# Issuing the products of two matrix stages in turn, one by one, in a retention-attention and two-layer feed-forward kernel

## The chip, the cores and the metric

The kernel runs on one core of one Trainium2 chip. The metric is the device time of one execution in microseconds, as the median of three runs.

## What is computed

The reference is a decayed causal attention (4 batches, 8 heads, 576 positions, 64 dimensions a head) followed by two feed-forward layers over its 2304 rows of 512 numbers. All operands come as float32 or float64 arrays and the result is float32.

```python
ret = scores * Dmat                      # scale * q k^T, times gamma**(i-j) for j <= i
x = (ret @ v) as (2304, 512)
h = x @ w_in1;  g = where(h > 0, h, exp(min(h, 0)) - 1);  x = g @ w_out1    # 512 -> 2048 -> 512
h = relu(x @ w_in2);                                      out = (h * h) @ w_out2
```

## The kernel before

The 2304 rows are cut into five token blocks (512, 512, 512, 256 and 512 rows). Each layer goes over the blocks, and in each block over 16 slices of 128 of the 2048 inner columns. One pass over one slice of one block is a step, so there are 160 steps, 80 in each layer.

A float32 product is made of three matrix products on float32r parts: each operand is a pair (hi, lo), and `mm3` (L104 to L107) issues hi times hi, hi times lo and lo times hi, all added up in one PSUM tile.

A step has these parts:

- `up` (L270) multiplies the block's input x with 128 columns of the first matrix. Four pieces of the inner dimension by three products make 12 products, all into one PSUM tile `h`, which is one bank. There are two buffers for `h`.
- The elementwise work on `h`. In layer 0, ACT takes a relu, an exp and a tanh (L283 to L285), DVE combines them (L287, L288), ACT rounds the result to the hi part of g (L101) and DVE subtracts it for the lo part (L102). In layer 1 it is one ACT relu (L290), one DVE product (L292) and the same two for the split. g has four buffers.
- `down1` or `down2` (L296, L310) multiplies g with 128 rows of the second matrix and adds that up, over all 16 slices of the block, in four PSUM tiles `acc` (two for the block of 256 rows in layer 1). These are 12 products: four tiles by three, the three of one tile one behind the other. The step's `down` is that of the step two back (`LAG = 2`, L26).
- At a block's last slice each `acc` tile is read out. In layer 0, ACT and DVE split it into a tile `x2`, which takes one of the four g buffers until a DMA has stored it. In layer 1 it is copied to a tile `o` and stored.

Products that write 512 columns are those of the four large blocks and all of `down2`; the rest write 256.

Between the ACT and the DVE part of the elementwise work, `mid` (L404) puts work that belongs to later steps: pieces of the next block's attention (its small products run on PE), and the conversion of the float64 weights to pairs of float32r (ACT, DVE and GpSimd). The first layer's weights are converted during the first block, the second layer's in blocks 1 to 3, and these are fetched and split again in block 4.

The order in which `tile_kernel` names the instructions is a priority and not yet the order of an engine's queue. The context is opened with `schedule_with_timeline_sim=True`, and its planner may take a later instruction first when it expects an earlier one to have to wait. On the chip each engine then runs its queue in the planned order. The lines that set the priority around the change are these:

```python
        up(layer, blk, f, mid)
        pend.append((layer, blk, f))
        if len(pend) > LAG:
            l, bb, ff = pend.pop(0)
            (down1, down2)[l](bb, ff)
```

Of the kernel before, what the change touches and what calls it, by code (L numbers as in the profile page):

```python
# [16 lines left out]
B, H, S, D = 4, 8, 576, 64  # L17
NT, DM, DFF = B * S, H * D, 2048
P = 128
NP = H // 2  # L20
KC = DM // P
# [3 lines left out]
NB = len(BLOCKS)  # L25
LAG = 2  # L26
WARM = 3
# What the upper word's magnitude becomes at most: what stays finite in float32r after the shift.
MOST = float(np.array([0x7F7FF000 >> 3], np.uint32).view(np.float32)[0])
# columns of the constants: identity, causal mask, then the scales of q and of k from each first position on  # L30
C_ID, C_MASK, C_S = 0, 128, 256


def chunks_of_blocks():
    """Per token block: (batch, first position, length), chunks of at most 128 positions that
    cross neither a batch nor a block."""
    out = []
    for t, n in BLOCKS:
        end, cs = t + n, []
        while t < end:  # L40
            b, s = divmod(t, S)
            n = min(P, S - s, end - t)
            cs.append((b, s, n))
            t += n
        out.append(cs)
    return out
# [11 lines left out]
def constants():  # L58
    """The decay between positions i and j is gamma**(i - j) = gamma**(i - S/2) * gamma**(S/2 - j):
    q has the first factor and k the second, so that states and scores need none."""  # L60
    c = np.zeros((P, C_ALL), np.float64)
    i = np.arange(P)
    gamma = 1.0 - 2.0 ** (-5.0 - np.arange(H))
    c[:, C_ID:C_ID + P] = np.eye(P)
    c[:, C_MASK:C_MASK + P] = i[:, None] <= i[None, :]
    for s in STARTS:
        e = (s + i - S // 2)[:, None].astype(np.float64)
        cq, ck = scale_cols(s)
        c[:, cq:cq + H] = gamma[None, :] ** e / np.sqrt(D)
        c[:, ck:ck + H] = gamma[None, :] ** -e  # L70
    return c.astype(np.float32)
# [3 lines left out]
def tile_kernel(ctx: ExitStack, tc, q, k, v, w_in1, w_out1, w_in2, w_out2, cst, out):  # L75
# [21 lines left out]

# [1 line left out]
    def split(pair_hi, pair_lo, src, eng=nc.vector):  # L99
        """src = hi + lo, each within float32r."""  # L100
        nc.scalar.copy(pair_hi, src)  # L101
        eng.tensor_tensor(out=pair_lo, in0=src, in1=pair_hi.bitcast(F32), op=ALU.subtract)  # L102
# [5 lines left out]

# [1 line left out]
    raws, f32s, w_t = {}, {}, {}  # L110
# [13 lines left out]
    def to_f32(u):  # L124
        """Round to float32: the upper word's magnitude moves up by three bits, the exponent's
        bias changes, and the sign and the rounded lower word are added to that."""
        raw = raws.pop(u)
        upper, lower = raw[:, :, 1], raw[:, :, 0]
        a = f_p.tile([P, DM], F32, tag="f", name="f")
        ai = a.bitcast(I32)  # L130
        nc.scalar.activation(lower, lower.bitcast(U32), AF.Copy, scale=2.0 ** -29)
        nc.scalar.activation(a, upper.bitcast(F32), AF.Abs, scale=2.0 ** -112)
        nc.vector.tensor_scalar_min(a, a, MOST)  # L133
        nc.vector.tensor_scalar(out=ai, in0=ai, scalar1=3, scalar2=None, op0=ALU.logical_shift_left)  # L134
        nc.vector.scalar_tensor_tensor(  # L135
            out=ai, in0=upper, scalar=-(1 << 31), in1=ai, op0=ALU.bitwise_and, op1=ALU.bitwise_or
        )
        nc.gpsimd.tensor_tensor(out=ai, in0=ai, in1=lower, op=ALU.add)  # L138
        f32s[u] = a
# [14 lines left out]

# [1 line left out]
    nat, spare = {}, {}  # L156
    x_t = {}
    blocks = chunks_of_blocks()
    chunks = [(ch, blk) for blk in range(NB) for ch in blocks[blk]]
    # chunks of the first block beside each other, in the places of weights that come late  # L160
    aside = blocks[0][1:4]
# [17 lines left out]
    def scale_chunk(ch):  # L179
        n = ch[2]  # L180
        qn, kn, _ = nat[ch]
        # VectorE converts weights during the first two blocks
        eng = nc.gpsimd if ch in blocks[0] + blocks[1] else nc.vector
        for t, c in zip((qn, kn), scale_cols(ch[1])):
            eng.tensor_tensor(
                out=t[:n], in0=t[:n], in1=cs[:n, c:c + H].unsqueeze(2).to_broadcast([n, H, D]), op=ALU.mult
            )

    def attn_pieces(ch, blk):
# [9 lines left out]
        def sbuf(name):  # L199
            if ch not in aside:  # L200
                # P1 comes when kT has been used
                return a_p.tile([P, NP, P], F32, tag="kT" if name == "P1" else name, name=name)
            return spare[ch][("qT", "kT", "P0", "P1").index(name) + 3].rearrange("s (p i) -> s p i", p=NP)
# [28 lines left out]
        def values():  # L232
            qT = live["qT"]
            _, kn, vn = nat[ch]
            ps = psum("ps_o")
            # one bank, cleared by its first product alone: the order counts
            for p in range(NP if s else 0):
# [26 lines left out]

# [1 line left out]
    g_t = {}  # L266
    acc_t = {}
    mark = [None]

    def up(layer, blk, f, mid):  # L270
        n = BLOCKS[blk][1]
        x = x_t[layer * NB + blk]
        w = w_t[layer, 0, f]
        h = ps_h.tile([P, TB], F32, tag="h", name="h")[:, :n]
        for c in range(KC):
            o = slice(c * P, (c + 1) * P)
            mm3(h, w[:, 0, o], w[:, 1, o], x[:, c, 0, :n], x[:, c, 1, :n], c == 0, c == KC - 1)
        t = t_p.tile([P, TB], F32, tag="t", name="t")[:, :n]
        g = g_p.tile([P, 2, TB], F32R, tag="g", name="g")
        if layer == 0:  # L280
            # exp(m) - 1 = (exp(m) + 1) * tanh(m / 2), which loses no digits near 0; never less than m
            e = t_p.tile([P, TB], F32, tag="e", name="e", bufs=1)[:, :n]
# [13 lines left out]
    def down1(blk, f):  # L296
        n = BLOCKS[blk][1]
        g, w = g_t.pop((blk, f)), w_t[0, 1, f]
        if f == 0:
            acc_t[blk] = [ps_acc.tile([P, TB], F32, tag="acc", name=f"acc{m}") for m in range(KC)]  # L300
        for m in range(KC):
            c = slice(m * P, (m + 1) * P)
            a = acc_t[blk][m][:, :n]
            mm3(a, w[:, 0, c], w[:, 1, c], g[:, 0, :n], g[:, 1, :n], f == 0, f == NF - 1)
            if f == NF - 1:
                x2 = g_p.tile([P, 2, TB], F32R, tag="g", name="x2")[:, :, :n]
                split(x2[:, 0], x2[:, 1], a)
                nc.sync.dma_start(out=x2s[blk][:, m], in_=x2.bitcast(F32))

    def down2(blk, f):  # L310
        t0, n = BLOCKS[blk]
        g, w = g_t.pop((blk, f)), w_t[1, 1, f]
        if f == 0:
            acc_t[blk] = [ps_acc.tile([P, DM], F32, tag="acc", name=f"acc{m}") for m in range(n // P)]
        for m in range(n // P):
            c = slice(m * P, (m + 1) * P)
            mm3(acc_t[blk][m], g[:, 0, c], g[:, 1, c], w[:, 0], w[:, 1], f == 0, f == NF - 1)
            if f == NF - 1:
# [9 lines left out]

    # the order in which the steps need the units of a layer
    units = [(0, 0)] + [u for f in range(NF) for u in ([(0, f + 1)] if f + 1 < NF else []) + [(1, f)]]  # L330
# [4 lines left out]
    nc.vector.memset(st, 0.0)  # L335
    # brings the tensor engine to its full clock while the first loads come in
    warm = ps_h.tile([P, 512], F32, tag="h", name="warm")
# [34 lines left out]
    def w1_step(n):  # L372
        """Units of the first layer's weights: n more loaded, then converted, then split."""
        for _ in range(n):
# [3 lines left out]

    # the first block's attention, its first two chunks side by side
    new_x(0)  # L380
# [22 lines left out]
    for i, (layer, blk, f) in enumerate(steps):  # L403
        def mid():  # L404
            if layer == 0 and blk < NB - 1:
                # the attention of the next block, spread over this one
                need = 3 * len(blocks[blk + 1])
# [6 lines left out]
            elif layer == 0 and i >= NF and at["f322"] < min(len(w2), (i - NF + 1) * 0.7):  # L414
                # the second layer's weights, as float32 in DRAM until there is room
                step("park", at["f322"], w2, park_w)
# [4 lines left out]

        up(layer, blk, f, mid)
        pend.append((layer, blk, f))
        if len(pend) > LAG:
            l, bb, ff = pend.pop(0)
            (down1, down2)[l](bb, ff)
        if at["f322"] == len(w2):
            step("park", 99, w2, park_w)
        # the second layer's weights take the first's places as its last block goes by
        j = i - (NB - 1) * NF  # L430
        if j >= 0:
            while at["split2"] < len(w2):
# [5 lines left out]
                step("split2", 99, w2, split_w)  # L438
        # the second layer's inputs
        if (layer, f) == (0, 1) and blk == NB - 1 or (layer, f) == (1, LAG) and blk < NB - 1:  # L440
# [3 lines left out]
    for l, bb, ff in pend:  # L444
        (down1, down2)[l](bb, ff)

# [25 lines left out]
```

## Time and profile before

| | |
|---|---|
| median of three runs | 928.78 us |
| lowest and highest run | 927.87 us, 930.71 us |
| profiled execution: span from its first to its last instruction | 926.7 us |
| median less that span | 2.1 us |
| PE busy with products | 895.6 us (97% of the span) |
| DVE busy | 488.0 us (53%) |
| ACT busy | 420.5 us (45%) |
| POOL (GpSimd) busy | 138.0 us (15%) |

The profile gives the profiled execution by its span alone; what lies around the span is taken as the 2.1 us to the median. A product's row lasts longer than the time until the next product starts, because products are pipelined. The pitch, from one start to the next, is what a product costs when the engine is full.

### The profile page before, as it was taken

The numbers are of one execution on the slowest core, as the hardware profiler recorded it, in microseconds if no ns is written. First come the engines' busy times: TensorE is split into PE (matmuls) and PEld (weight loads), VectorE is DVE, ScalarE is ACT, GpSimd is POOL, SyncE is SP. The second block draws the span as 40 slices with busy tenths as digits, with TensorE's granted clock in tenths as the row PEclk, the third lists the DMA queues.
The fourth block names the chain that finished last, engine by engine and source line by source line (L and its number), as shares of the span: only waits on it lengthen the run. The fifth ranks groups of instructions, "written<-read, shape, count | busy, mean of one in ns | idle before, by whom it ended". The sixth has DMA issues, their size and how long they took to land.

```text
span 926.7 us, 12546 instructions
## 1 busy us (share of the span) xinstructions
PE 895.6 (97%) x4934; PEld 741.2 (80%) x4934; DVE 488.0 (53%) x784; ACT 420.5 (45%) x762; POOL 138.0 (15%) x102
## 2 busy tenths in 40 slices
PE   6988788999999999999999999999999999999997
PEld 4766566878888888999888888888888888988886
DVE  4799999676656655776566542232223222323222
ACT  4576676665556565665666532222222222222221
POOL 4565555121111111211000000000000000000000
PEclk9999999999999999999999999999999999999999
DMA  9752555274434533663443420030002002100001
GB/s 227 180 159 93 159 150 158 65 230 127 113 100 173 137 91 107 220 176 122 150 126 92 159 91 1 1 137 1 0 1 91 1 1 82 55 2 23 1 1 45
DMA packets 94778, 89.09 MB, mean 96 GB/s; under 512 B 59008, under 2 KB 77568, under 8 KB 94208
## 3 DMA queue, kind: packets, MB, share of 16 engines
q1 hardware_dynamic: 94720, 88.30, 32.2%
q8 instruction: 38, 0.62, 0.3%
q14 instruction: 20, 0.16, 0.1%
HBM read 65.74 MB, written 22.54 MB: 95 GB/s over the span
## 4 chain that ended last, share of the span: by engine, by line
PE 83%; DVE 11%; issue 2%; ACT 1%; DMA 1%; POOL 1%; SPq 0%; DVEq 0%; ACTq 0%
PE acc L105 13%; PE acc L106 13%; PE acc L107 13%; PE h L105 13%; PE h L106 13%; PE h L107 13%; DVE f L133 2%; DVE f L135 2%; DVE t L287 2%; PE ps_o L242 2%; DVE f L134 1%; PE ps_s L223 1%; PE ps_t L210 1%; PE ps_o L238 1%; DVE w L102 1%
## 5 line engine op out<-in xcount | busy, mean ns | idle before, releaser
L105 PE MATMUL h<-x,w 128*128 128x512 f32 (+1 forms) x640 | 238.3, 373 | 6.5 <-DVE t L288 5.8
L107 PE MATMUL h<-x,w 128*128 128x512 f32 (+1 forms) x640 | 237.8, 372 | 1.9 <-DVE w L102 1.9
L106 PE MATMUL h<-x,w 128*128 128x512 f32 (+1 forms) x640 | 237.1, 371 | 0.0
L292 DVE SCALAR_TENSOR_TENSOR t<-h,t 128x512 f32<-128x512 f32 (+1 forms) x80 | 51.1, 639 | 229.9 <-ACT t L290 229.9
L290 ACT ACTIVATE t<-h 128x512 f32<-128x512 f32 (+1 forms) x80 | 44.5, 556 | 237.1 <-PE h L107 237.1
L101 ACT CAST g<-t 128x512 fp32r<-128x512 f32 (+1 forms) x160 | 92.4, 578 | 128.0 <-DVE t L288 65.2
L105 PEld LDWEIGHTS h<-x,w 128*128 128x128 f32 x640 | 121.3, 190 | 29.8 <-ACT e L284 3.8
L102 DVE TENSOR_TENSOR g<-t,g 128x512 fp32r<-128x512 f32 (+1 forms) x160 | 108.7, 679 | 66.3 <-ACT g L101 59.4
L107 PEld LDWEIGHTS h<-x,w 128*128 128x128 f32 x640 | 121.2, 189 | 24.7 <-DVE w L102 4.4
L106 PEld LDWEIGHTS h<-x,w 128*128 128x128 f32 x640 | 121.4, 190 | 21.1 <-DVE x L102 0.4
L138 POOL TENSOR_TENSOR f<-f,raw 128x512 int32<-128x512 int32 x64 | 94.2, 1472 | 270.6 <-DVE f L135 186.1
L106 PE MATMUL acc<-g,w 128*128 128x512 f32 (+1 forms) x320 | 119.3, 374 | 2.5 <-DVE g L102 2.5
L105 PE MATMUL acc<-g,w 128*128 128x512 f32 (+1 forms) x320 | 116.8, 381 | 4.9 <-ACT g L101 4.8
L107 PE MATMUL acc<-g,w 128*128 128x512 f32 (+1 forms) x320 | 118.1, 370 | 0.0
L105 PE MATMUL acc<-w,g 128*128 128x512 f32 x288 | 112.2, 390 | 0.0
L106 PE MATMUL acc<-w,g 128*128 128x512 f32 x288 | 112.2, 390 | 0.0
L107 PE MATMUL acc<-w,g 128*128 128x512 f32 x288 | 111.6, 389 | 0.0
L287 DVE SCALAR_TENSOR_TENSOR t<-e,t 128x512 f32<-128x512 f32 (+1 forms) x80 | 60.0, 750 | 53.6 <-ACT t L285 53.1
L105 PEld LDWEIGHTS acc<-g,w 128*128 128x128 f32 x320 | 60.0, 190 | 16.9 <-ACT g L101 5.7
L283 ACT ACTIVATE t<-h 128x512 f32<-128x512 f32 (+1 forms) x80 | 44.3, 554 | 60.6 <-PE h L107 59.6
L106 PEld LDWEIGHTS acc<-g,w 128*128 128x128 f32 x320 | 60.5, 189 | 13.8 <-DVE g L102 4.0
L107 PEld LDWEIGHTS acc<-g,w 128*128 128x128 f32 x320 | 60.4, 189 | 10.1
(62 smaller groups left out, 954.8 us busy)
## 6 DMA issues: line engine op xcount, KB each, us to landing
raw<-in_moe_w_in_dram SPq DMA_DIRECT2D x32, 512.0 KB, 4.2
raw<-in_moe_w_out_dram SPq DMA_DIRECT2D x32, 512.0 KB, 3.6
x2s<-x SPq DMA_DIRECT2D x16, 512.0 KB, 3.3
w2s<-f SPq DMA_DIRECT2D x32, 256.0 KB, 2.3
f<-w2s SPq DMA_DIRECT2D x32, 256.0 KB, 2.7
x<-x2s SPq DMA_DIRECT2D x4, 2048.0 KB, 7.9
out_dram<-o SPq DMA_DIRECT2D x18, 256.0 KB, 2.1
q<-in_q_dram SPq DMA_DIRECT2D x13, 256.0 KB, 4.3
```

Of the source, the lines that this page charges most:

```text
L101: nc.scalar.copy(pair_hi, src)
L102: eng.tensor_tensor(out=pair_lo, in0=src, in1=pair_hi.bitcast(F32), op=ALU.subtract)
L105: nc.tensor.matmul(ps, l_hi, r_hi, start=first, stop=False)
L106: nc.tensor.matmul(ps, l_hi, r_lo, start=False, stop=False)
L107: nc.tensor.matmul(ps, l_lo, r_hi, start=False, stop=last)
L133: nc.vector.tensor_scalar_min(a, a, MOST)
L135: nc.vector.scalar_tensor_tensor(out=ai, in0=upper, scalar=-(1 << 31), in1=ai, op0=ALU.bitwise_and, op1=ALU.bitwise_or)
L138: nc.gpsimd.tensor_tensor(out=ai, in0=ai, in1=lower, op=ALU.add)
L283: nc.scalar.activation(t, h, AF.Relu, scale=-1.0)
L287: nc.vector.scalar_tensor_tensor(out=t, in0=e, scalar=1.0, in1=t, op0=ALU.add, op1=ALU.mult)
L290: nc.scalar.activation(t, h, AF.Relu)
L292: nc.vector.scalar_tensor_tensor(out=t, in0=h, scalar=0.0, in1=t, op0=ALU.max, op1=ALU.mult)
```

## The change

`up` and the two `down` functions no longer issue their products one stage behind the other. Each makes a list, and a new function `interleave` issues one product of the step's `up`, then one of the `down` of two steps back, and so on: 12 and 12, or 12 and 6 in layer 1's block of 256 rows, where every second `up` product is followed by a `down` product. A product of `down` stands between any two of `up`, and the other way round.

Inside a `down` list the order is new as well. It was tile by tile (hi hi, hi lo, lo hi of tile 0, then of tile 1, and so on). It is now part by part: hi times hi of all tiles, then hi times lo of all, then lo times hi of all, so that neighbours in the list alone (after the last step, where no `up` is left) write different tiles too.

The read-out of the accumulators at a block's last slice moves to `out1` and `out2`, called after all of the step's products and after the elementwise work of its `up` and `mid`. The elementwise work and `mid` stand behind the step's 24 products, where they stood between its 12 of `up` and its 12 of `down`. The products themselves, their number, shapes and operands are the same, as are all buffers. Removed comments are left out of the diff.

```diff
+PARTS = ((0, 0), (0, 1), (1, 0))
...
+    def interleave(ups, downs):
+        n = max(len(ups), len(downs))
+        for k in range(n):
+            for of in (ups, downs):
+                for ps, l, r, first, last in of[k * len(of) // n:(k + 1) * len(of) // n]:
+                    nc.tensor.matmul(ps, l, r, start=first, stop=last)
+
-    def up(layer, blk, f, mid):
+    def up(layer, blk, f, mid, downs):
...
+        ups = []
         for c in range(KC):
             o = slice(c * P, (c + 1) * P)
-            mm3(h, w[:, 0, o], w[:, 1, o], x[:, c, 0, :n], x[:, c, 1, :n], c == 0, c == KC - 1)
+            for i, j in PARTS:
+                ups.append((h, w[:, i, o], x[:, c, j, :n], (c, i, j) == (0, *PARTS[0]), (c, i, j) == (KC - 1, *PARTS[-1])))
+        interleave(ups, downs)
...
     def down1(blk, f):
...
-        for m in range(KC):
-            c = slice(m * P, (m + 1) * P)
+        return [
+            (acc_t[blk][m][:, :n], w[:, i, m * P:(m + 1) * P], g[:, j, :n], f == 0 and (i, j) == PARTS[0], f == NF - 1 and (i, j) == PARTS[-1])
+            for i, j in PARTS for m in range(KC)
+        ]
+
+    def out1(blk, f):
+        n = BLOCKS[blk][1]
+        for m in range(KC if f == NF - 1 else 0):
             a = acc_t[blk][m][:, :n]
-            mm3(a, w[:, 0, c], w[:, 1, c], g[:, 0, :n], g[:, 1, :n], f == 0, f == NF - 1)
-            if f == NF - 1:
+            if True:
                 x2 = g_p.tile([P, 2, TB], F32R, tag="g", name="x2")[:, :, :n]
...
     def down2(blk, f):
...
+        return [
+            (acc_t[blk][m], g[:, i, m * P:(m + 1) * P], w[:, j], f == 0 and (i, j) == PARTS[0], f == NF - 1 and (i, j) == PARTS[-1])
+            for i, j in PARTS for m in range(n // P)
+        ]
+
+    def out2(blk, f):
+        t0, n = BLOCKS[blk]
         for m in range(n // P):
-            c = slice(m * P, (m + 1) * P)
-            mm3(acc_t[blk][m], g[:, 0, c], g[:, 1, c], w[:, 0], w[:, 1], f == 0, f == NF - 1)
             if f == NF - 1:
...
-        up(layer, blk, f, mid)
         pend.append((layer, blk, f))
-        if len(pend) > LAG:
-            l, bb, ff = pend.pop(0)
-            (down1, down2)[l](bb, ff)
+        done = pend.pop(0) if len(pend) > LAG else None
+        up(layer, blk, f, mid, (down1, down2)[done[0]](*done[1:]) if done else [])
+        if done:
+            (out1, out2)[done[0]](*done[1:])
...
     for l, bb, ff in pend:
-        (down1, down2)[l](bb, ff)
+        interleave([], (down1, down2)[l](bb, ff))
+        (out1, out2)[l](bb, ff)
```

## Rows read from the trace of the kernel before

**Rows 1.** The page: span, and busy time of each engine.

```profile
span 926.7 us, 12546 instructions
...
PE 895.6 (97%) x4934; PEld 741.2 (80%) x4934; DVE 488.0 (53%) x784; ACT 420.5 (45%) x762; POOL 138.0 (15%) x102
```

**Rows 2.** Windows of 23 us: window and its length, busy us by engine, granted clock, DMA.

```profile
46.00:69.00 23.00, 20.27 (x126) 15.18 (x124) 22.82 (x31) 16.79 (x31) 14.06 (x10) 1.00 0.57 159
...
161.00:184.00 23.00, 23.00 (x115) 18.79 (x114) 14.30 (x23) 13.61 (x24) 4.39 (x4) 0.99 0.20 53
...
874.00:897.00 23.00, 23.00 (x104) 19.03 (x103) 5.54 (x8) 4.88 (x8) 0.00 (x0) 1.00 0.00 1
```

**Rows 3.** Waits of PE between 40 and 161 us: total us, times, longest.

```profile
PE h L105 <- DVE t L288: 5.8, 6, 1.5
```

**Rows 4.** Groups of products by line and shape: count, busy us, mean ns.

```profile
L105 PE MATMUL h<-x,w 128*128 128x512 f32 x512 | 201.7, 394 | 6.5 <-DVE t L288 5.8 <-ACT e L284 0.4 <-ACT t L283 0.2
...
L105 PE MATMUL acc<-w,g 128*128 128x512 f32 x288 | 112.2, 390 | 0.0
...
L105 PE MATMUL acc<-g,w 128*128 128x512 f32 x256 | 99.4, 405 | 4.9 <-ACT g L101 4.8
...
L105 PE MATMUL h<-x,w 128*128 128x256 f32 x128 | 36.6, 286 | 0.0
...
L105 PE MATMUL acc<-g,w 128*128 128x256 f32 x64 | 17.4, 287 | 0.0
```

**Rows 5.** Timeline, a step of layer 1: start us, us; first products of three runs.

```profile
702.48 0.39 PE L105 MATMUL h<-x,w 128*128 128x512 f32 x1
...
705.20 0.39 PE L105 MATMUL acc<-w,g 128*128 128x512 f32 x1
...
707.92 0.39 PE L105 MATMUL h<-x,w 128*128 128x512 f32 x1
```

**Rows 6.** Timeline, the last four products of the kernel.

```profile
920.78 1.07 PE L107 MATMUL acc<-w,g 128*128 128x512 f32 x4
```

**Rows 7.** Timeline, products of 256 columns in `down1` of block 3.

```profile
440.72 0.52 PE L105 MATMUL acc<-g,w 128*128 128x256 f32 x3
...
441.80 0.28 PE L105 MATMUL acc<-g,w 128*128 128x256 f32 x1
...
442.04 0.28 PE L107 MATMUL acc<-g,w 128*128 128x256 f32 x1
```

**Rows 8.** Timeline, layer 0, block 4: a step's last `h` product, its g's hi part.

```profile
498.26 0.39 PE L107 MATMUL h<-x,w 128*128 128x512 f32 x1
...
502.47 0.62 ACT L101 CAST g<-t 128x512 fp32r<-128x512 f32 x1 [0.45 <-DVE t L288]
```

**Rows 9.** Groups by line: the longest of three DVE instructions that convert a weight unit.

```profile
L135 DVE SCALAR_TENSOR_TENSOR f<-raw,f 128x512 int32<-128x512 int32 x64 | 46.7, 730 | 0.6
```

**Rows 10.** As rows 8, in layer 0, block 3 (256 columns).

```profile
436.42 0.28 PE L107 MATMUL h<-x,w 128*128 128x256 f32 x1
...
438.97 0.41 ACT L101 CAST g<-t 128x256 fp32r<-128x256 f32 x1 [0.95 <-DVE t L288]
```

**Rows 11.** As rows 8, in layer 1, block 4.

```profile
913.30 0.39 PE L107 MATMUL h<-x,w 128*128 128x512 f32 x1
...
915.14 0.62 ACT L101 CAST g<-t 128x512 fp32r<-128x512 f32 x1 [0.76 <-DVE t L292]
```

**Rows 12.** Timeline (PE's, then ACT's), end of layer 0's first block.

```profile
176.89 0.39 PE L107 MATMUL acc<-g,w 128*128 128x512 f32 x1
...
183.88 0.39 PE L105 MATMUL acc<-g,w 128*128 128x512 f32 x1
...
181.21 1.07 ACT L101 CAST x<-acc 128x512 fp32r<-128x512 f32 x2
...
188.46 0.58 ACT L101 CAST x<-acc 128x512 fp32r<-128x512 f32 x1
```

**Rows 13.** DMA issues on the page: count, size each, median us to landing.

```profile
x2s<-x SPq DMA_DIRECT2D x16, 512.0 KB, 3.3
```

## The prediction

> **What bounds the kernel now.** The page comes first. PE is busy for 97% of the span and no other engine for more than 53% [rows 1]. A share of busy time is a mean over stages, so the windows come next. They show two stages. From 46 to about 161 us DVE is busy for 22.82 of 23 us, and PE has gaps: the first layer's weights are being converted, and DVE sets the pace. From 161 us on PE is busy for all 23 us of a window, DVE for 14.3 us and later for 5.5, at a granted clock of 0.99 to 1.00, which is the 2.4 GHz level [rows 2]. There PE sets the pace, and the view of waits has no row for PE after 161 us. Before it, PE's largest wait is 5.8 us in six pieces, for the DVE instruction that frees an `h` buffer [rows 3].
>
> So a change in the order of PE's products can act in three ways: on the pitch of a product, which counts for 766 us of the span; on waits that PE does not have now; and on DVE's pace in the first stage.
>
> The third view is the timeline, because a pitch is read from starts and not from busy times. In a step of layer 1, twelve `h` products, all into one bank, start at 702.48 us, and the twelve `acc` products behind them at 705.20; those write four banks, three products each. The next step starts at 707.92 [rows 5]. Both runs last 2.72 us, which is 227 ns a product.
>
> **The change part by part.**
>
> *The pitch.* The number and shapes of the products stay: by count 3 x (512 + 288 + 256) = 3,168 of 512 columns and 3 x (128 + 64) = 576 of 256 columns [rows 4]. What the change alters is that neighbours write different banks. The kernel before already has such neighbours, which is the row to look for. Within the run of `h` products no neighbours differ in bank, within the run of `acc` products three of eleven pairs do, and both runs last 2.72 us to the hundredth [rows 5]. If a change of bank saved 13 ns, the second run with its entry into a new bank would be about 0.05 us shorter. The last four products of the kernel are better still: the planner has put the last part of all four `acc` tiles one behind the other, so each writes another bank than its neighbour. They take 1.07 us together; less the 0.39 us of one row [rows 11], three pitches are 0.68 us, or 227 ns each [rows 6]. With 256 columns, three products into three banks take 0.52 us, less 0.28 that is two pitches of 120 ns; two pitches inside one bank, from 441.80 to 442.04, are 120 ns too [rows 7]. So the price of a change of bank is read as 0, and I take 0 for all 3,744 products.
>
> How far could it go? From 256 to 512 columns the pitch grows by 107 ns, or 0.42 ns a column, so 13 ns of a pitch do not depend on the columns. No order of the products can save more than that. Outside the first block (16 steps of 24 products, in the stage that DVE paces) 3,744 - 384 = 3,360 products remain, and 3,360 x 13 ns = 44 us is the end of the range downwards. The other end is 0 as well: no row shows a bank change that costs.
>
> The Trainium skill, in TensorE: Matmul & The Clock Gate, section Back-to-back issue gap, puts the pitch at the columns over 2.4 GHz plus 2.5 ns, about 216 ns for 512 columns, and names no bank. The rows, at 227 ns, do not agree with that figure, so something here takes 11 ns more; if it were the bank, an estimate by this page is 11 ns for each product behind the first block, some 35 us less.
>
> *The time that g has.* Before, 48 products lie between the end of a step's `h` and the first product that reads its g. Now `h` ends with the 23rd of its step's 24 products, one `down` product and the 24 of the next step follow, then one `up` product, and then the first product on g. From the start of the last `h` product that is 27 pitches: 6.13 us at 512 columns and 3.24 at 256, where it was 49 pitches or 11.1 us. This halves the time for the elementwise chain, which counts wherever PE is the bound. The rows give the chain. In layer 1 the hi part is ready 915.14 + 0.62 - 913.30 = 2.46 us after that start [rows 11]: 3.7 us to spare in most of 80 steps, cost 0. In block 4 of layer 0 it takes 502.47 + 0.62 - 498.26 = 4.83 us [rows 8]: 1.3 us to spare, cost 0. In block 3 it takes 438.97 + 0.41 - 436.42 = 2.96 us against 3.24 [rows 10]: 0.28 us to spare, just enough. The lo part is one DVE instruction more, near 0.73 us [rows 9], and is first read eight products (1.8 us) later. The `h` buffer is asked for again one pitch before g, and the cast that ends the chain no longer reads it.
>
> In blocks 1 to 3, ACT and DVE also do the attention and convert 32 weight units. One conversion holds DVE for at most 3 x 0.73 = 2.2 us [rows 9], which is 0.9 us more than the spare 1.3. Uncovered, that is 32 x 0.9 = 29 us. What covers it is the attention's own work on PE, which lies between `h` and g too, and the planner, which moves other products forward. I take 0 and keep 29 as an end.
>
> *The first stage.* Now `h` ends up to 12 products (2.72 us) later, as it is mixed with products that wait for g. On DVE, the conversions of later units stand in the queue meanwhile, and DVE is full [rows 2]. So I take 0. Without that cover it would be 16 x 2.72 = 44 us; a better fit of the two engines could at most give back PE's 5.8 us [rows 3].
>
> *The read-out of a layer-0 block.* Four `acc` tiles go through four g buffers to DRAM. Before, the tiles ended one after another, and PE did 7 us of other work, from the last product at 176.89 to the next `acc` product at 183.88, while ACT read the tiles from 181.21 to 188.46 [rows 12]. Now the four end within the step's last seven products, the first one 0.7 us later than before, and the next block's products on the same banks stand at once between those of `up`. The third tile needs a g buffer back: a cast of 0.58 [rows 12] and a DVE instruction near 0.73 [rows 9] for the first tile, 3.3 for its store [rows 13] and 1.3 again make 5.9 us, or 4.6 us after the step's end, as the first tile is ready 1.36 us ahead of it. PE's ready work meanwhile is 12 `up` products and 6 on the first two tiles (4.1 us) and in most blocks a piece of attention. What remains is 0 to 1 us if the planner moves these forward, as it did before, and 4.6 - 5 x 0.227 = 3.5 us if it doesn't, since the sixth product in the new order is the one on the third tile. Four block ends lie inside layer 0 and one at its end: 0 to 17 us; I take 0.4 each, 2 us, nearest to the row of before, where PE lost nothing. On SP the stores stand behind the loads of `mid`, as before.
>
> *The end.* The last products are already one part of four tiles in a row [rows 6], so the tail stays: 0.
>
> *Sum.* 926.7 + 0 (pitch) + 0 (chains) + 0 (first stage) + 2 (block ends) = 928.7, and with 2.1 us around it 930.8 us, against a median of 928.78. I say 931.
>
> **The rivals.**
>
> *The bank costs something after all* (4%). It takes a cost that shows only when every neighbour differs. Against it stand four different banks in a row at 227 ns [rows 6]. It would give 929 - 44 = 885 us.
>
> *The first stage fits better* (12%). The planner makes a new order for all engines; if PE's 5.8 us [rows 3] mostly go before 161 us, the time is about 925 us. For it speaks that this wait is for the `h` buffer and that products of `down` now come in earlier; against it that DVE is full there, so that PE's gaps are not what sets the time.
>
> *PE waits for g* (24%). This is the slower side: one product of `down` whose g or bank is late holds all `up` products behind it, where before twelve of them were ahead. It decides when the chain exceeds 27 pitches, in layer 0 beside conversions and at block ends. With half of the 29 us and 1 us at each of five block ends it is 929 + 14 + 5 = 948; with a third of both, 940. The Trainium skill, TensorE: Matmul & The Clock Gate, section Step-by-step: what each phase is for, says that matmuls keep program order and only weight loads are pulled ahead. The wait in rows 3 agrees.
>
> *The change doesn't do what it says.* If the planner undoes the alternation, the queue is nearly the old one and the time 929; this lies inside the forecast.
>
> **How the numbers follow.** The forecast, no change in pitch and a few microseconds of new waits, has 60%: 927 to 936 us. A measurement of this kernel tells 0.3%, or 2.8 us, from no change. Of the 60%, 42 lie within that and 18 above it. Slower is then 18 + 24 = 42%, faster 12 + 4 = 16%, same 42%. The range from 925 to 945 leaves out the bank's case, most of the far half of the wait for g, and a little on each side.
>
> **What would show it.** The pitch after is 227 and 120 ns in the steps of layer 1, with `h` and `acc` rows in turn, and a step of layer 1 lasts 24 x 0.227 = 5.44 us as before. PE's waits after 161 us, if any, name ACT's or DVE's g or the reading of `x2`, and lie in layer 0. DVE stays full until about 161 us. The prediction is wrong if the pitch falls towards 214 ns, or if block 3 and the block ends together lose over 10 us.

## The result, and the profile after

The changed kernel takes 936.32 us (median of 4 runs) against 929.75 us for the kernel before, measured beside it: a ratio of 1.007 with a 95% interval from 1.0056 to 1.0085. It is 0.7% slower. The execution that was profiled first took 3,130 us, with every product of PE slowed down for its whole length; it is left out of the ratio (the median of the other three is 936.14 us), and the profile shown from here on is of another execution of the same kernel (the run `after_again`, 936.78 us), in which everything runs at its usual speed.

The page of the changed kernel: span, busy time.

```profile
span 935.0 us, 12564 instructions
...
PE 904.4 (97%) x4934; PEld 745.7 (80%) x4934; DVE 488.0 (52%) x784; ACT 417.9 (45%) x762; POOL 137.4 (15%) x102
```

Against [rows 1] the span is 8.3 us longer, and so is PE's busy time (8.8 us). DVE's is the same to 0.1 us. PE does not idle more; it is busy longer with the same 4,934 products. Of the 8.8 us, 3.2 lie ahead of 161 us (134.8 us of PE's work before, 138.0 after), where DVE sets the pace, so not all of them are loss. The windows answer to [rows 2]:

```profile
46.00:69.00 23.00, 20.83 (x128) 16.30 (x127) 22.70 (x31) 17.02 (x30) 14.09 (x10) 0.99 0.55 158
161.00:184.00 23.00, 23.00 (x125) 18.37 (x124) 13.02 (x21) 11.82 (x21) 2.99 (x3) 0.96 0.15 38
...
874.00:897.00 23.00, 23.00 (x104) 19.03 (x103) 5.53 (x8) 5.09 (x9) 0.00 (x0) 1.00 0.00 1
```

The picture by stage is the old one: DVE full up to 161 us, then PE full. In the last window PE has 104 products, as before. From 164 to 926 us the granted clock is 1.00 in both kernels, so a lower clock has no part in what is lost behind the first block.

**Pitch.** The timeline of PE in a step of layer 1, which answers to [rows 5]:

```profile
701.14 0.39 PE L278 MATMUL h<-x,w 128*128 128x512 f32 x1
701.37 0.39 PE L278 MATMUL acc<-w,g 128*128 128x512 f32 x1
701.60 0.39 PE L278 MATMUL h<-x,w 128*128 128x512 f32 x1
...
703.86 0.39 PE L278 MATMUL h<-x,w 128*128 128x512 f32 x1
704.09 0.39 PE L278 MATMUL acc<-w,g 128*128 128x512 f32 x1
...
704.77 1.07 PE L278 MATMUL h<-x,w 128*128 128x512 f32 x4
705.68 0.62 PE L278 MATMUL acc<-w,g 128*128 128x512 f32 x2
```

`h` and `acc` stand in turn. From 701.14 to 703.86 there are twelve products, each into another bank than its neighbours, and they take 2.72 us, which is 227 ns each and the same as twelve into one bank. At the step's end the planner has put four `h` products together (704.77), so even here not all neighbours differ. The trace of all of layer 1 has 1,005 pairs of 512 columns that change between `h` and `acc`, with a mean pitch of 227 ns, and 241 pairs that stay in one `h` bank, with 227 ns as well.

**Where the time went.** The start of the last `down` product of each layer-0 block marks the block's end. The times between these starts, in us, and the time from the last one to the last `down` product of layer 1, for the runs of this study:

| run | first block | block 1 | block 2 | block 3 | block 4 | layer 1 |
|---|---|---|---|---|---|---|
| before | 176.9 | 105.6 | 96.4 | 67.3 | 87.4 | 387.8 |
| changed (`after_again`) | 178.2 | 107.5 | 100.1 | 67.3 | 88.3 | 387.8 |
| `list_order_only` | 176.5 | 105.6 | 96.4 | 67.7 | 87.4 | 387.8 |
| `layer1_only` | 177.9 | 105.6 | 96.4 | 67.3 | 87.4 | 387.8 |
| `not_first_block` | 175.8 | 110.1 | 100.1 | 67.2 | 88.3 | 387.8 |
| `attention_steps_b12` | 178.4 | 106.8 | 100.0 | 66.5 | 87.4 | 387.8 |
| `no_attention_steps` | 182.4 | 107.1 | 97.5 | 67.5 | 88.2 | 387.8 |
| `half_in_turn` | 180.1 | 106.9 | 98.5 | 68.2 | 87.5 | 388.1 |
| `short_old` | 174.4 | 106.5 | 95.8 | 67.1 | 87.0 | 387.8 |
| `short_turn` | 176.0 | 106.2 | 98.0 | 67.7 | 87.0 | 387.8 |
| `kept_whole` | 193.3 | 115.5 | 106.9 | 76.2 | 96.9 | 393.2 |
| `whole_mid` | 176.9 | 113.2 | 101.0 | 66.3 | 88.3 | 387.8 |
| `whole_old` | 180.1 | 113.0 | 103.4 | 67.3 | 87.4 | 387.8 |

Each row is one profiled execution. `before`, `list_order_only` and `layer1_only` plan layer 0 almost alike, and their first blocks end between 176.5 and 177.9 us, so 1 us there says little. Of the changed kernel's 7.7 us up to the end of layer 1, 1.3 stand in the first block, 1.9 in block 1, 3.7 in block 2, 0.9 in block 4, and nothing in block 3 and in layer 1's 80 steps.

**Waits.** PE's waits after 161 us, where the kernel before has none (total us, times, longest):

```profile
PE ps_o L240 <- DVE P L228: 1.1, 2, 0.9
PE h L278 <- DVE t L301: 1.0, 1, 1.0
```

The second is at the end of block 3, in the timeline at 457.10 us: `up` of the next step stands behind DVE's release of its `h` buffer.

```profile
456.35 0.69 DVE L301 TENSOR_TENSOR t<-h,t 128x512 f32<-128x512 f32 x1
456.64 0.61 ACT L103 CAST w<-f 128x512 fp32r<-128x512 f32 x1
457.10 3.04 PE L278 MATMUL h<-x,w 128*128 128x512 f32 x12 [0.98 <-DVE t L301]
```

That is block 4's 0.9 us. The first, for `P`, is two waits in block 3, which as a whole lasts as long as before. Named waits make 2.1 us together, and none of them is in blocks 1 and 2: what these lose, 5.6 us, has no wait beside it.

**Attention's stretches.** It shows when PE's products are taken by kind. A stretch is a run of attention products with a wide product (`h` or `acc`) on either side; its cost is the time from the start of the last wide product ahead to the start of the second one behind, less two pitches. Between 164 and 460 us the kernel before has 43 stretches with 637 products, which cost 49.0 us. The changed one has 50 with 632, which cost 55.0. That is 6 us for fewer products, 1.1 of it the wait for `P` above. In blocks 1 and 2 alone the stretches cost 29.9 us before (26 of them) and 35.0 us after (34), which is 5.1 of the 5.6 us that these blocks lose. A whole set of scores in the kernel before (PE's timeline):

```profile
317.84 0.39 PE L107 MATMUL h<-x,w 128*128 128x512 f32 x1
318.15 0.68 PE L223 MATMUL ps_s<-qT,kT 64*64 64x64 f32 x16
318.77 0.50 PE L105 MATMUL acc<-g,w 128*128 128x512 f32 x1
319.11 0.39 PE L106 MATMUL acc<-g,w 128*128 128x512 f32 x1
```

and the scores of the same size in the changed kernel:

```profile
300.80 1.52 PE L278 MATMUL acc<-g,w 128*128 128x512 f32 x6
302.25 0.56 PE L225 MATMUL ps_s<-qT,kT 64*64 64x64 f32 x10
302.74 1.66 PE L278 MATMUL acc<-g,w 128*128 128x512 f32 x6
304.24 2.88 PE L278 MATMUL h<-x,w 128*128 128x512 f32 x12
307.05 0.44 PE L225 MATMUL ps_s<-qT,kT 64*64 64x64 f32 x6
307.42 1.89 PE L278 MATMUL acc<-g,w 128*128 128x512 f32 x7
```

The first costs 319.11 - 317.84 - 2 x 0.227 = 0.82 us. In the second, ten are issued, then 18 wide products, then the other six, at 0.69 + 0.57 = 1.26 us. Entering and leaving is what costs: in the fence of the kernel before the wide product ahead takes 0.31 us to the next start, the last scores 0.15 (0.2 in sets of 128 columns), and the first wide product behind them 0.34 instead of 0.227. So this cut costs 0.44 us. One cut of the larger sets of 128 columns costs 0.6 us (1.29 whole, 1.06 + 0.83 in two). The transposes of q and k (`ps_t`) are another case: eight in one stretch cost 0.87 us (changed kernel, 426.21 us), four and four in two stretches 0.44 each (kernel before, 422.10 and 422.78 us), so that a cut there costs nothing.

### The profile page after: what moved, and what is told of

Its sections match the earlier page's. It is cut to its first block, busy times and chain, and to the rows that moved or that the text cites. A ratio compares the mean times of both kernels' runs of the same rounds, so it can differ in the third digit from the quotient of the medians.

```text
span 3128.7 us, 12564 instructions
## 1 busy us (share of the span) xinstructions
PE 3121.7 (100%) x4934; PEld 1794.8 (57%) x4934; DVE 475.0 (15%) x784; ACT 416.7 (13%) x762; POOL 129.5 (4%) x102
## 4 chain that ended last, share of the span: by engine, by line
PE 100%; DVE 0%; ACT 0%; issue 0%
PE acc L278 46%; PE h L278 45%; PE ps_s L225 2%; PE ps_o L244 2%; PE ps_t L212 2%; PE ps_o L240 2%; PE ps_u L254 1%; PE warm L362 0%; DVE o L344 0%; ACT spare L217 0%; ACT kT L217 0%; DVE st L358 0%
## 5 line engine op out<-in xcount | busy, mean ns | idle before, releaser
L278 PE MATMUL h<-x,w 128*128 128x512 f32 (+1 forms) x1920 | 1695.7, 1007 | 0.0
L278 PEld LDWEIGHTS h<-x,w 128*128 128x128 f32 x1920 | 821.5, 443 | 598.6 <-issue 586.5
L278 PE MATMUL acc<-w,g 128*128 128x512 f32 x864 | 863.4, 1094 | 0.0
L278 PE MATMUL acc<-g,w 128*128 128x512 f32 (+1 forms) x960 | 837.5, 1010 | 0.0
L278 PEld LDWEIGHTS acc<-g,w 128*128 128x128 f32 x960 | 418.2, 455 | 294.2 <-issue 282.6
L278 PEld LDWEIGHTS acc<-w,g 128*128 128x128 f32 x864 | 371.6, 432 | 317.2 <-issue 313.9
L225 PEld LDWEIGHTS ps_s<-qT,kT 64*128 64x128 f32 (+1 forms) x272 | 48.6, 458 | 26.6 <-issue 16.0
L225 PE MATMUL ps_s<-qT,kT 64*128 64x128 f32 (+1 forms) x272 | 55.0, 531 | 0.7 <-ACT kT L217 0.7
L244 PE MATMUL ps_o<-P,v 128*64 128x128 f32 (+1 forms) x272 | 54.6, 585 | 0.0
L301 DVE TENSOR_TENSOR t<-h,t 128x512 f32<-128x512 f32 (+1 forms) x80 | 50.8, 634 | 1.7
```

Source lines behind the costliest of these rows:

```text
L225: nc.tensor.matmul(ps[e][:n, p, :n], kT[r, p, :n], qT[r, p, :n], start=True, stop=True)
L244: nc.tensor.matmul(ps[e * D:(e + 1) * D, p, :n], vn[:n, 2 * p + e, :], live[e][:n, p, :n], start=not s, stop=True, skip_group_check=True,)
L278: nc.tensor.matmul(ps, l, r, start=first, stop=last)
L301: nc.vector.tensor_tensor(out=t, in0=h, in1=t, op=ALU.max)
```

## The experiments

Twelve kernels ran. Their edits are shown against the changed kernel, shortened; ratios are to the kernel before, measured beside each. The first four ask which part of the change and which stage loses.

**after_again**: the changed kernel as it is.

> The changed kernel once more, for a profile at PE's usual speed. New waits of PE (theory A): the pitch in layer 1 is 227 ns, a layer-1 step lasts 5.44 us, and PE has waits after 161 us that name g, h or x2 in layer 0 and sum to 4 to 8 us. A longer pitch (theory B): the pitch is 228.5 to 229 ns everywhere. The first stage (theory C): the first block's last down ends 4 to 8 us later than the 176.9 us of before, and all later stages last as long as before.

Measured: 936.78 us, the rows above. The pitch and layer 1 are as theory A has them, which leaves B out; the named waits, 2.1 us, are too few for A as it stands, and the first block's 1.3 us are too little for C.

**layer1_only**: products in turn where a function `in_turn` says so, else the old path.

```diff
+    def in_turn(layer, blk, f):
+        return layer == 1
...
+        if in_turn(layer, blk, f):
+            up(layer, blk, f, mid, (down1, down2)[done[0]](*done[1:]) if done else [])
...
+        else:
+            up(layer, blk, f, mid, [])
+            if done:
+                (old1, old2)[done[0]](*done[1:])    # the old down1 and down2
```

> Products in turn in layer 1's 80 steps alone, layer 0 in the old order. Theory A (waits in layer 0): within 1 us of the kernel before. Theory B (a longer pitch): half of the loss, about 3 us slower. Theory C (first stage): within 1 us of before.

Measured: 929.38 us against 928.83, ratio 1.0004 (0.9991 to 1.0017). Products in turn in half of all steps change nothing that can be told, for better or worse: the interval leaves at most 1.6 us, under 2 ns for each added change between `h` and `acc`, as the price of a change of bank.

**not_first_block**: the same with `in_turn = (layer, blk) != (0, 0)`.

> Products in turn everywhere but in the first block's 16 steps. Theory A: 4 to 7 us slower than before, nearly the whole loss. Theory B: about 6 us slower. Theory C: within 1 us of before.

Measured: 936.19 us, ratio 1.0081 (1.0061 to 1.0102). The whole loss is there without the first block, so it arises in blocks 1 to 4 of layer 0, where A has it. The border between the first two blocks moves, though: the first one ends 1.1 us earlier than before, more of the attention is left behind it (257 products in block 1, against 232 before and 236 in the changed kernel), and block 1 takes 4.5 us longer. From block 2 on the times are the changed kernel's.

**list_order_only**: `in_turn` false everywhere, but with the new list order and the late read-out.

```diff
-                (old1, old2)[done[0]](*done[1:])
+                interleave([], (down1, down2)[done[0]](*done[1:]))
+                (out1, out2)[done[0]](*done[1:])
```

> The new order inside the down list and the late read-out alone: the step's 12 products of up stay ahead of its 12 of down. Theory A: 0 to 2 us slower, what the block ends cost; the rest of the loss is the time that g has. Theory B: about 2 us slower, since neighbours write other banks in half the products. Theory C: within 1 us of before.

Measured: 929.13 us, ratio 1.0002 (0.9991 to 1.0012). The order within the list and the late read-out cost nothing, at block ends neither.

The next four were sent with theory B in a new sense, the cutting of the attention.

**no_attention_steps**: `in_turn = layer == 1 or blk == NB - 1 or f >= NF - 3`.

> Products in turn only in steps without attention: layer 1, the last block of layer 0, and the last three steps of its other blocks. Theory A: 1 to 3 us slower than before, for block 4 has the longest chain of the steady steps, against the least time. Theory B: within 1 us of before.

Measured: 939.18 us, ratio 1.01 (1.0079 to 1.0121). Neither theory had this. By the table 5.5 us are in the first block, of which only the last three steps are in turn; 1.5 in block 1, 1.1 in block 2, 0.8 in block 4. A mixed order is planned anew in the first stage too. What it loses there no run tells apart; the granted clock over the first 180 us is 0.92 in this run and 0.96 before, so a lower clock may be part of it.

**attention_steps_b12**: `in_turn = layer == 0 and blk in (1, 2) and f < NF - 3`.

> Products in turn only in the 26 steps of blocks 1 and 2 of layer 0 that have attention pieces between them. Theory A: 2 to 5 us slower than before, by waits of PE that the profile names. Theory B: 4 to 7 us slower with hardly a named wait, and more stretches of attention in those blocks.

Measured: 932.65 us, ratio 1.0033 (1.002 to 1.0046): 3 us slower, at the lower end of A and below B's 4. By the table blocks 1 and 2 lose 4.8 us of the changed kernel's 5.6, and block 3 is 0.9 us shorter. Between 164 and 460 us there are 46 stretches, which cost 52.3 us for the 637 products, 3.2 more than before, and the largest named wait of PE in these blocks is 1.0 us. So 26 steps of 160 carry near half of the whole loss, and most of that of their own blocks.

**half_in_turn**: `down` products start half a list later.

```diff
-        for k in range(n):
-            for of in (ups, downs):
-                for ... in of[k * len(of) // n:(k + 1) * len(of) // n]:
+        late = n // 2 if ups and downs else 0
+        for k in range(n + late):
+            for of, j in ((ups, k), (downs, k - late)):
+                for ... in of[j * len(of) // n:(j + 1) * len(of) // n] if 0 <= j < n else []:
```

> The down products start six products of up later: six of up alone, six and six in turn, six of down alone. From the last h product to the first product on its g there are then 37 pitches, between the 27 of the changed kernel and the 49 of before. Theory A: at most half of the loss is left, 929.5 to 932.5 us. Theory B: the planned order has 71 stretches of attention as the changed kernel's has (65 before), so the loss stays, 934 to 937 us.

Measured: 938.97 us, ratio 1.01 (1.0078 to 1.0121), outside both. By the table, blocks 1 and 2 lose 3.4 us where products fully in turn lose 5.6, as A has it; but 3.2 us are in the first block. It has 51 stretches, which cost 51.9 us: as many as the changed kernel's and 3 us cheaper. The number of stretches alone does not say what they cost; what is cut does, as the account of the prediction below shows.

**kept_whole**: an attention piece is bound behind the step's last product, and the next step's products behind the piece.

```diff
+        with tc.issue_after(tail[0]):       # around the products of a step
...
+        tail[0] = i.ins
...
+            with tc.issue_after(tail[0]):   # around an attention piece
                 todo.pop(0)()
+            tail[0] = last_pe[0]
```

> The changed order, with the planner bound to keep a piece of the attention's products whole: a piece comes behind the last product of the step before it, and the next step's products behind the piece's last one. Theory A (PE waits because g and h come too late for products in turn): no gain, since PE can dodge a wait even less: 936 us or slower. Theory B (the attention's small products are cut into more stretches, 50 instead of 43 between 164 and 460 us, and each entry and exit costs): the loss goes, 926 to 931 us.

Measured: 990.46 us, ratio 1.0654 (1.063 to 1.0678). The time is on A's side, but the binding takes more from the planner than was meant, in every block. PE's waits between 30 and 470 us:

```profile
PE acc L286 <- DVE x L104: 19.2, 8, 4.4
PE h L286 <- DVE t L310: 11.5, 4, 5.1
PE ps_o L243 <- DVE P L231: 5.9, 1, 5.9
```

The largest sum, which no theory named, is the block end: products on an `acc` bank wait until DVE has split the old tile (`x`), up to 4.4 us at a time.

The last four were meant to part the two readings: h and g are late, and the planner fills the gap with attention (A); or the new order cuts the attention whatever is late (D).

**whole_mid**: the binding only in steps 3 to 12 of blocks 1 and 2. **whole_old**: the same binding, `up` ahead of `down` as before, but with the new order within the `down` list, which `list_order_only` shows to cost nothing where nothing is bound.

> The changed order, with attention pieces bound to stay whole only in steps 3 to 12 of blocks 1 and 2, away from block ends and from the first stage. Theory A: what was filled with attention is now a wait of PE, 934 to 942 us, and the profile names waits of PE for h or g in blocks 1 and 2. Rival D (a cut costs by itself and nothing is late): 929 to 932 us.

> The same binding in the same steps with the old order of products (up first, then down). Theory A: with 49 pitches nothing is late, so binding costs nothing, and up to 1.5 us of stretches may be saved: 927.5 to 930 us, no waits of PE for h or g there. Rival D: the same.

Measured: `whole_mid` 941.73 us, ratio 1.0134 (1.012 to 1.0149); `whole_old` 943.31 us, 1.0154 (1.0138 to 1.0171). The control fails: binding costs the old order as much. So `whole_mid` tells nothing on cuts, though its time lies where A had it. What it costs stands in PE's timeline of `whole_old` at the end of block 1:

```profile
297.74 1.65 PE L286 MATMUL acc<-g,w 128*128 128x512 f32 x6 [0.49 <-DVE x L104]
302.09 1.21 PE L286 MATMUL acc<-g,w 128*128 128x512 f32 x3 [2.70 <-DVE x L104]
304.52 1.65 PE L286 MATMUL acc<-g,w 128*128 128x512 f32 x3 [1.23 <-DVE x L104]
```

```profile
290.00:313.00 23.00, 18.58 (x83) 14.14 (x82) 11.26 (x20) 11.68 (x21) 2.90 (x2) 0.85 0.48 166
```

Step 3 may not pass step 2's last products, which stand on banks that are still being read. PE waits 4.4 us in three pieces, and the granted clock of that window is 0.85: from 303 to 309 us it is 0.50, the 1.2 GHz level.

**short_turn** and **short_old**: layer 0 with layer 1's elementwise work.

```diff
-        if layer == 0:
+        if layer == 2:                       # both layers take the short branch
...
-            nc.scalar.activation(t, h, AF.Relu)
+            mark[0] = nc.scalar.activation(t, h, AF.Relu).ins
```

> Both layers get layer 1's elementwise work (relu squared, one ACT and one DVE instruction ahead of the split), so exp, tanh and two DVE instructions of layer 0 are left out; products in turn as in the changed kernel. To be read against short_old. Theory A (h and g come too late for 27 pitches, and the planner fills the gap with attention products, which cuts these): with a chain of about 2.5 us instead of 4.8 nothing is late, and it is within 1.5 us of short_old. Rival D (products in turn break up the attention whatever the chain is, since the planner has more places to cut): 5 to 8 us slower than short_old.

> The same shortened elementwise work in layer 0 with the old order of products. Some microseconds faster than the kernel before in the first stage, where DVE has less to do; both theories give the same for it, it is the measure for short_turn.

Measured: `short_turn` 928.99 us (ratio to the kernel before 0.9996, 0.9986 to 1.0005), `short_old` 924.81 us (0.995, 0.9936 to 0.9963). In turn is 4.2 us slower with the short chain, where it is 6.6 with the long one: between the two expectations. By the table, block 4 loses nothing where the changed kernel lost 0.9, and blocks 1 and 2 together lose 2.0 where it lost 5.6, 1.1 of the 2.0 as one named wait of PE for g; block 3 loses 0.6 and the first block 1.6. So the larger part of what blocks 1, 2 and 4 lose goes with the elementwise work of layer 0. That this is the length of the chain is likely but not parted from its load, since the short branch also takes instructions off ACT and DVE.

## Why the prediction was right, and where it was off

The forecast was 931 us, with slower and the same at 42% each, and a range from 925 to 945 us; 936.3 lies in it. That it does is owed in part to the width of the range: the sum forecast 2 us of loss, for block ends, and 6.6 us were measured, most of them from a term that stood at 0.

*The pitch: right, and shown.* Where neighbours differ, the pitch is 227 ns as in [rows 5, 6], and layer 1 takes 387.8 us before and after. `layer1_only` at 1.0004 is the test of it by itself. The 13 ns beside the columns have another cause, which no run here shows.

*The time that g has: right in kind, not in number.* From the start of the last `h` product to the first product on its g, 27 pitches or 6.13 us were reckoned. In layer 1 it is 6.8 us, because the planner puts four `h` products together at the step's end. In block 4 of layer 0 it is 8.6 to 10.2 us in the steady steps, where it was 11.1. There the planner takes the alternation back in every other step (PE's timeline):

```profile
481.28 0.39 PE L278 MATMUL h<-x,w 128*128 128x512 f32 x1
481.50 0.39 PE L278 MATMUL acc<-g,w 128*128 128x512 f32 x1
481.73 2.88 PE L278 MATMUL h<-x,w 128*128 128x512 f32 x12
484.45 2.88 PE L278 MATMUL acc<-g,w 128*128 128x512 f32 x12
```

Of 383 pairs of wide products that follow each other, `h` and `acc` change places in 255 in block 1, 243 in block 2 and 117 in block 4; it was 31 in each before. In layer 0 the change does only in part what it says, which was among the rivals.

*The cover by attention: the step that failed.* The prediction put conversions and late g in blocks 1 to 3 at 0, because "what covers it is the attention's own work on PE" and the planner. The cover is real, as PE is full and only 2.1 us of waits have a name. But it was taken as free, and it isn't. Near the end of block 2 the changed kernel shows how it is used:

```profile
365.76 0.69 DVE L301 TENSOR_TENSOR t<-h,t 128x512 f32<-128x512 f32 x1
...
366.48 0.62 ACT L103 CAST g<-t 128x512 fp32r<-128x512 f32 x1 [1.48 <-DVE t L301]
...
368.66 0.93 PE L225 MATMUL ps_s<-qT,kT 64*128 64x128 f32 x10
...
369.52 0.96 PE L278 MATMUL h<-x,w 128*128 128x512 f32 x3
...
370.33 0.85 PE L278 MATMUL acc<-g,w 128*128 128x512 f32 x3
...
375.19 0.71 PE L225 MATMUL ps_s<-qT,kT 64*128 64x128 f32 x6
```

Ten of the sixteen scores stand ahead of three `h` and three `acc` products, and the other six come at 375.19 us. The `h` products needed the buffer that DVE had let go at 366.45 us, and the `acc` products the g that ACT had finished at 367.10: both were there 3 us ahead. So on the chip nothing was late at this cut. The same holds all over blocks 1 and 2, where `h`'s buffer is free at least 1.1 us ahead of a step's first `h` product and g's hi part ready at least 1.5 us ahead of its first use. A plan that puts attention where it expects a wait would look like this, but no run shows its estimates, so why it cuts here is argued and not shown.

What the cuts cost is shown. Blocks 1 and 2, without the stretches that hold transposes alone:

| run | stretches | products | cost, us | PE's waits in them, us |
|---|---|---|---|---|
| before | 17 | 344 | 23.7 | 0 |
| changed (`after_again`) | 26 | 362 | 29.4 | 0 |
| `half_in_turn` | 23 | 340 | 26.7 | 0 |
| `no_attention_steps` | 22 | 344 | 26.2 | 0 |
| `attention_steps_b12` | 20 | 354 | 27.5 | 1.2 |
| `short_old` | 17 | 344 | 24.2 | 0 |
| `short_turn` | 19 | 344 | 25.6 | 1.1 |

Five more stretches cost 2.5 us in `no_attention_steps` and six more 3.0 us in `half_in_turn`, which is 0.5 us for each and agrees with the two cuts measured above. The nine more of the changed kernel would be 4.5 us by that price (an estimate), and the 18 more products in them come on top; together they cost 5.7 us, which is the loss of these two blocks. The stretches of transposes alone are 9 before and 12 in `half_in_turn`, and cost 6.2 us in both. With the short chain only two stretches come on top instead of nine. The term "chains" had 0 in the sum where 5 to 6 us belong, still far below its upper end of 29 us.

*Block ends: right in kind, a little high.* 2 us were taken. `list_order_only` shows that the late read-out costs nothing, and the one named wait at a block end is 1.0 us, at the start of block 4. What it would be without the planner's freedom was put at 3.5 us a block end; `whole_old` has 4.4 us of waits at one such end, and a lower clock behind them.

*The first stage: within what the runs can tell.* DVE is as full as before up to 161 us, and `not_first_block`, which has its first block in the old order, is as slow as the changed kernel. In the profiled execution the first block is 1.3 us longer, about as much as it differs between kernels that plan it almost alike. But `no_attention_steps` shows that this stage can move by 5 us when only the last steps are planned anew, more than the 0 in the sum allows for.

**What stays open.** `short_turn` still loses 4.2 us with a chain that leaves time to spare, 2.6 of it outside the first block. Rival D, by which a list in turn is cut whatever the chain, has little room there: two cuts and one wait are all that blocks 1 and 2 show. Whether the planner cuts with the long chain because of its own estimate of that chain, or because ACT and DVE have more to do, was not parted: the binding that should have tested the cuts cost more than what it was to measure.

## What to carry to other kernels

Before removing a supposed neighbour cost, look for neighbours in the old trace that already have the new form: here a few rows said that a change of bank is worth nothing. Where two stages are put in turn, count what the first stage's end moves behind, since the time for the work between them shrinks even if no engine idles. And filler work on a full engine is not free: cutting a set of scores or values in two cost half a microsecond here, so a plan that hardly waits can still be slower.

## What was not expected of the hardware

A set of small float32 products (scores, values) that is cut in two by wide products costs 0.44 us (64 columns) to 0.6 us (128 columns) more than in one piece: the last small product holds the next wide one by 0.15 to 0.2 us, and the first wide product behind takes 0.34 us to the next start instead of 0.227. A cut set of transposes costs nothing. After waits of PE of a few microseconds, as in `whole_old`, the products from 305.12 to 308.96 us start every 0.43 us, while the granted clock is 0.50.
